# Gated mix of a 2D spectral filter and a Mish MLP: W read once and copied on chip, loads on three queues, half of w1 ahead of later x, larger butterflies, new cost numbers in its build-time planner

## Chip, cores and metric

The kernel runs on one core of a Trainium2 chip. The metric is device microseconds of one execution, as the median of several runs. The profile's span is 1.7 us shorter than the time of the same run (164.8 against 166.51 us before). Runs of this one-core program are called fast or slow by their time against the fastest of the same kernel; each run also lists the mean granted TensorE clock.

## Reference

Input x is 2048 x 512 in bf16. The output is `g * a + (1 - g) * b`:

```python
g = sigmoid((x * gate_w).sum(-1, keepdims=True))
a = irfft2(rfft2(x) * (w_r + 1j * w_i))            # W is 2048 x 257, real and imaginary
b = mish(x @ w1 + b1) @ w2                         # w1 512 x 1792, w2 1792 x 512
# reference() takes B_x too, but calls the MLP with A_x
```

## The kernel before

All transforms are matmuls. x is transposed on TensorE (`tr`), butterflies (sums and differences of halves of a tile) on VectorE or GpSimd feed the row transform (`a1`, with matrix FD), the first column stage (`s1`, with FT) follows, and its result goes through DRAM scratch `scr1` (four writes `r1w`, four reads `r1r`) to be regrouped. Then comes the second stage `s2`, the product with W on VectorE, and the way back (SM, GT and GD are the matrices of these stages). A DMA is issued by an engine into its own queue: `sp` is SyncE, `act` ScalarE, `pool` GpSimd. The MLP is `mm1` (56 groups of four 512-column matmuls, the activation function Mish on ScalarE after each) and `mm2`.

Nothing is ordered at run time. Each step is a task; a small planner in the kernel simulates the engines at build time with cost numbers and a priority per task, and writes one fixed instruction list per engine. Each engine works through its list in order. If the planner believes that W arrives early, it places W's first use early, and TensorE then stands still there.

```python
free = {e: 0.0 for e in ENGS}                       # in schedule(): when each engine is free
...
def dma(name, dst, src, nbytes, ..., queue="sp", bw=DMA_BW):       # DMA_BW = 390e3 bytes/us
    t = G.add(name, [(queue, 0.1, lambda e: e.dma_start(dst, src))], ...)   # an issue costs 0.1 us
    t.xfer = nbytes / bw                            # all transfers one after the other
...
# W into Wa/Wb [128, 32, 257]: both halves of the partitions hold the same values
def wload(nm, dst, src_t, o, cos, wdep):
    for co in (cos,):
        base = 64 * co
        ...  # p: 32 rows of 16448 B; r, n, s: rows of 514 B in reversed order
for t in range(NT):
    ...
    if t % 4 == 3:
        t_r1w.append(dma(f"r1w{t // 4}", scr1_w[...], A1s[...], ...))
        wload(*((("wr", Wa, ...), ("wi", Wb, ...))[t // 8]), (t // 4) % 2, list(t_r1w[-1].deps))
...
G.add("tab", ..., reads=WA + WB + ["SM"], ...)      # first TensorE use of W
G.add("z", ..., reads=IN2 + ["SM"], ...)            # needs all four scr1 reads
G.add(f"s2_{gp}", ..., reads=[("In2", gp // 4), "SM"], ...)   # needs one of them
G.add(f"hs_{c}_{ft}", ..., reads=[sl, "b1f", "gth"], ...)     # Mish only after the gate
```

## Time and profile before

| | before |
|---|---|
| timed, first three runs | 168.49 us (167.88 to 169.06) |
| profiled span | 164.8 us |
| TensorE busy | 137.2 us |
| longest TensorE wait | 13.89 us |
| DMA bytes | 22.78 MB |

From the page of the profile, the busy tenths of TensorE, the granted TensorE clock in tenths and the DMA engines' share, each in 40 slices of 4.12 us:

```profile
PE   1397998693002999999999999999999999999991
PEclk9999999999655699999999999999999999999999
DMA  4798999999999993030303891100101000011011
```

TensorE has a hole in slices 10 to 13 and is full afterwards, so I read the kernel's end as TensorE's remaining work plus whatever idle time came before. The clock falls inside the hole and comes back only with the work after it. DMA is busy from about 6 to 60 us.

The timeline of TensorE (start in us, duration, engine, line, operation and tiles, count, and in brackets the idle time before and what ended it). L785 is mm1, L687 the first use of W, L733 the first use of scr1:

```profile
30.70 7.94 PE L785 MATMUL ps<-xT,w_sb 128*128 128x512 bf16 x36 [1.39 <-ACT hsb L793]
52.54 0.22 PE L687 MATMUL ps<-Wa,SM 128*128 128x32 bf16 x1 [13.89 <-DMA Wb<-in_A_w_i_dram]
...
53.21 0.39 PE L733 MATMUL ps<-R,SM 128*128 128x256 bf16 x1 [0.19 <-DMA R<-scr]
```

36 matmuls are 9 mm1 groups; 4 more stood earlier. So 13 groups were done ahead of W's first use, and 43 of the 56 were still to come while TensorE waited. W came at 52.5 us, the first scr1 read at 53.2: both arrive together, so with this order, taking away only one of the two waits should gain next to nothing.

The same trace, SyncE's DMA issues from 28 us (the duration is the time the issue took):

```profile
28.23 0.47 SPq L480 DMA_DIRECT2D scr<-R  x1
28.74 6.41 SPq L480 DMA_DIRECT2D Wb<-in_A_w_i_dram  x4
...
36.18 0.36 SPq L480 DMA_DIRECT2D scr<-R  x1
36.59 7.71 SPq L480 DMA_DIRECT2D Wb<-in_A_w_i_dram  x4
45.83 1.81 SPq L480 DMA_DIRECT2D R<-scr  x4
```

The last scr1 write was issued at 36.18 us although its data was ready at 30.2: four Wb loads were before it in the list. The table of stretches (start:end, length, busy time and count of each engine, clock, DMA share, GB/s):

```profile
42.00:48.00 6.00, 0.00 (x0) 0.00 (x0) 0.00 (x0) 0.00 (x0) 0.00 (x0) 0.53 1.09 272
48.00:54.00 6.00, 1.08 (x10) 0.85 (x12) 0.38 (x2) 0.00 (x0) 0.00 (x0) 0.50 1.13 256
54.00:60.00 6.00, 5.97 (x27) 2.71 (x27) 4.23 (x14) 2.55 (x4) 0.00 (x0) 0.83 1.06 371
```

No engine computes from 42 to 48 us.

### The profile page before, as it was taken

What the parts mean: (1) busy time and instruction counts of PE and PEld (TensorE: products, weight loads), DVE (VectorE), ACT (ScalarE), POOL (GpSimd) and SP (SyncE); (2) the same over time, 40 slices, a digit from 0 to 9 for tenths busy, and PEclk for the clock granted to TensorE, in tenths of its full rate; (3) what the DMA queues carried; (4) which work ended last, traced back from release to release, by engine and by line L of the source; (5) the groups of instructions that cost most, each with busy time, mean ns of one, the idle gap of its engine ahead of it and who ended that gap; (6) DMA issues with size and microseconds to landing.
All of it is one profiled execution on the core that took longest, in us unless ns stands there. A gap on an engine that the chain in (4) does not pass through costs nothing.

```text
span 164.8 us, 2256 instructions
## 1 busy us (share of the span) xinstructions
PE 137.2 (83%) x835; PEld 72.3 (44%) x850; DVE 74.5 (45%) x172; ACT 76.4 (46%) x126; POOL 9.3 (6%) x16
## 2 busy tenths in 40 slices
PE   1397998693002999999999999999999999999991
PEld 0265667241001444444444475544566444444440
DVE  0288796300000869599630079207888500311311
ACT  3259876984000277865232768622359774000000
POOL 1082063000000000000000000000000000000000
PEclk9999999999655699999999999999999999999999
DMA  4798999999999993030303891100101000011011
GB/s 144 282 374 336 248 157 342 153 280 139 344 135 282 385 354 118 38 127 0 127 0 142 242 258 64 64 4 0 64 0 66 4 0 0 0 64 64 4 64 64
DMA packets 19615, 22.78 MB, mean 138 GB/s; under 512 B 916, under 2 KB 16404, under 8 KB 19476
## 3 DMA queue, kind: packets, MB, share of 16 engines
q1 hardware_dynamic: 19604, 22.63, 49.8%
q8 instruction: 7, 0.11, 0.3%
q14 instruction: 4, 0.03, 0.1%
HBM read 16.34 MB, written 6.29 MB: 137 GB/s over the span
## 4 chain that ended last, share of the span: by engine, by line
PE 76%; DMA 13%; ACT 4%; POOL 2%; issue 1%; SPq 1%; DVE 0%; POOLq 0%
PE ps L803 29%; PE ps L785 28%; DMA scr<-R 6%; DMA R<-scr 4%; PE ps L851 4%; DMA R<-in_A_x_dram 3%; PE ps L832 2%; PE ps L759 2%; PE ps L760 2%; PE ps L735 2%; PE ps L582 2%; ACT R L505 2%; POOL PX L602 1%; PE ps L659 1%; PE ps L637 1%
## 5 line engine op out<-in xcount | busy, mean ns | idle before, releaser
L785 PE MATMUL ps<-xT,w_sb 128*128 128x512 bf16 x220 | 53.5, 382 | 1.7 <-ACT hsb L793 1.4
L793 ACT ACTIVATE hsb<-ps,b1f 128x512 bf16<-128x512 f32 x56 | 37.9, 688 | 30.5 <-PE ps L785 30.1
L803 PE MATMUL ps<-w_sb,hsb 128*128 128x512 bf16 x218 | 49.7, 379 | 0.3
L803 PEld LDWEIGHTS ps<-w_sb,hsb 128*128 128x128 bf16 x224 | 21.8, 98 | 25.5
L785 PEld LDWEIGHTS ps<-xT,w_sb 128*128 128x128 bf16 x224 | 21.5, 99 | 24.1 <-ACT hsb L793 1.7
L505 ACT ACTIVATE R<-ps 128x512 bf16<-128x512 f32 (+1 forms) x29 | 16.8, 594 | 7.7 <-PE ps L760 5.0
L882 DVE SCALAR_TENSOR_TENSOR R<-ps,omg,R 128x512 bf16<-128x512 f32 x8 | 6.0, 751 | 26.0 <-PE ps L803 26.0
L504 DVE CAST R<-ps 128x512 bf16<-128x512 f32 (+1 forms) x19 | 12.8, 689 | 9.1 <-PE ps L760 6.2
L746 DVE TENSOR_TENSOR PX<-ps,Wa 128x256 bf16<-128x256 f32 x32 | 12.0, 416 | 0.6 <-PE ps L734 0.6
L582 PE MATMUL ps<-ident,R 128*128 128x128 bf16 x64 | 6.7, 264 | 6.6 <-DMA R<-in_A_x_dram 6.5
L746 DVE TENSOR_TENSOR PX<-ps,Wb 128x256 bf16<-128x256 f32 x32 | 12.0, 417 | 0.1
L687 PE MATMUL ps<-Wa,SM 128*128 128x32 bf16 x1 | 0.2, 217 | 13.9 <-DMA Wb<-in_A_w_i_dram 13.9
L813 ACT ACTIVATE R<-ps,omg 128x512 bf16<-128x512 f32 x8 | 5.5, 687 | 12.1 <-PE ps L803 12.1
L694 DVE COPY tz<-ps 128x64 f32<-128x64 f32 x1 | 0.2, 225 | 22.8 <-PE ps L690 22.8
L591 ACT ACTIVATE xT<-ps 128x512 bf16<-128x512 bf16 x12 | 6.6, 601 | 6.3 <-PE ps L582 6.2
L839 DVE CAST TT<-ps 128x512 bf16<-128x512 f32 x5 | 3.4, 690 | 12.9 <-PE ps L832 12.9
L851 PE MATMUL ps<-GD,TT 128*128 128x256 bf16 x64 | 9.1, 273 | 0.0
L859 DVE SCALAR_TENSOR_TENSOR PX<-ps,gcol,R 128x512 f32<-128x512 f32 x8 | 6.0, 744 | 6.8 <-ACT R L813 6.1
L582 PEld LDWEIGHTS ps<-ident,R 128*128 128x128 bf16 x64 | 5.1, 119 | 8.0 <-DMA R<-in_A_x_dram 7.0
L874 DVE SCALAR_TENSOR_TENSOR R<-ps,gcol,PX 128x256 bf16<-128x256 f32 x16 | 7.7, 482 | 1.2 <-ACT PX L865 0.8
L875 DVE SCALAR_TENSOR_TENSOR R<-ps,ngcol,PX 128x256 bf16<-128x256 f32 x16 | 7.6, 476 | 0.0
L851 PEld LDWEIGHTS ps<-GD,TT 128*128 128x128 bf16 x64 | 5.9, 98 | 3.6 <-ACT TT L842 1.3
(88 smaller groups left out, 105.9 us busy)
## 6 DMA issues: line engine op xcount, KB each, us to landing
scr<-R SPq DMA_DIRECT2D x8, 512.0 KB, 3.1
R<-scr SPq DMA_DIRECT2D x8, 512.0 KB, 7.4
w_sb<-in_B_w_dram SPq DMA_DIRECT2D x4, 896.0 KB, 11.8
out_dram<-R SPq DMA_DIRECT2D x8, 256.0 KB, 2.0
R<-in_A_x_dram SPq DMA_DIRECT2D x3, 512.0 KB, 6.5
Wa<-in_A_w_r_dram SPq DMA_DIRECT2D x2, 514.0 KB, 9.5
Wb<-in_A_w_i_dram SPq DMA_DIRECT2D x2, 514.0 KB, 11.2
SM<-c_sm SPq DMA_DIRECT2D x1, 640.0 KB, 8.8
```

Of the source, the lines that this page charges most:

```text
L504: G.add(name, [("dve", dve_dur(n), lambda e: e.tensor_copy(out=outf(), in_=inf())), ("act", act_dur(n), lambda e: e.activation(outf(), inf ...
L505: ("act", act_dur(n), lambda e: e.activation(outf(), inf(), AF.Copy))],
L582: ins = e.transpose(psb[:, bk(sl), 128 * dt_:128 * (dt_ + 1)], x_sb[:, t, 128 * dt_:128 * (dt_ + 1)], ident[:, :])
L591: return e.activation(xT[:, :, t, :], psb[:, bk(sl), 0:512].rearrange("p (a b) -> p a b", a=4), AF.Copy)
L746: ins = e.tensor_tensor(out=po, in0=px, in1=pw, op=ALU.mult)
L785: ins = e.matmul(ps[:, bk(sl), :], w1_sb[:, dt_, 128 * ft:128 * (ft + 1)], xT[:, dt_, 4 * c:4 * c + 4, :], start=(dt_ == 0), stop=(dt_ == 3))
L793: return e.activation(hsb[:, hb, ft, :], ps[:, bk(sl), :], AF.Mish, bias=b1f[:, ft:ft + 1])
L803: ins = e.matmul(ps[:, bk(sl), :], hsb[:, hb, ft, 128 * tl:128 * (tl + 1)], w2_sb[:, ft, :], start=(ft == 0), stop=(ft == NFT - 1))
L851: ins = e.matmul(ps[:, bk(sy), 256 * hh:256 * (hh + 1)], TT[:, st.i, i, :], GD[:, i, :], start=(i % 2 == 0), stop=(i % 2 == 1))
L859: return e.scalar_tensor_tensor(out=o, in0=ps[:, bk(sy), 0:256].unsqueeze(1).to_broadcast([128, 2, 256]), scalar=gcol[:, t:t + 1], in1=ya[ ...
L874: e.scalar_tensor_tensor(out=ya[:, t, 0:256], in0=ps[:, bk(sy), 256:512], scalar=gcol[:, t:t + 1], in1=tE[:, se.i, 0:256], op0=ALU.mult, o ...
L875: return e.scalar_tensor_tensor(out=ya[:, t, 256:512], in0=ps[:, bk(sy), 256:512], scalar=ngcol[:, t:t + 1], in1=hi, op0=ALU.mult, op1=ALU ...
```

## The change

The intent: read W from HBM once (2.1 instead of 4.2 MB) into partitions 0 to 63 and copy it to 64 to 127 on chip; put W, the stage matrices SM, w2, GD and GT on the GpSimd queue, so that scr1's writes don't stand behind them; split the first loads over SyncE and ScalarE; load half of w1 ahead of x's later tiles so that mm1 can start; make most butterflies over four tiles instead of two. The planner's cost numbers change too.

```diff
+BGRP = {1: (0, 2), 3: (2, 2), 7: (4, 4), 11: (8, 4), 15: (12, 4)}
-        free = {e: 0.0 for e in ENGS}
+        free = {e: 0.8 for e in ENGS}
-            t = G.add(name, [(queue, 0.1, lambda e: e.dma_start(dst, src))], ...
+            t = G.add(name, [(queue, {"sp": 0.46, "act": 0.46, "pool": 1.0}[queue], lambda e: ...)], ...
+        ld_x(0, 1)
+        dma("ld_fd", ..., queue="act")
+        ld_x(1, 4)
+        dma("ld_ft0", ..., queue="act")
+        ld_w1(0)
...  (b1, gate_w on "act"; then x 4 to 8, FT, x 8 to 16 on SyncE)
+        t_w1 = ld_w1(1)
+        def wload(nm, dst, src_t, o):       # partitions 0 to 63 only, deps=[t_w1], queue="pool"
...  (the rows of 514 B are planned with bw=130e3)
+        dma("ld_sm", ..., deps=[t_w1], queue="pool")    # likewise w2 and GD; GT after the last s1
+        for o, W in (("Wa", Wa), ("Wb", Wb)):
+            for h in range(2):
+                js = slice(16 * h, 16 * h + 16)
+                G.add(f"cp{o}{h}", [("dve", dve_dur(4112, 4), ... e.tensor_copy(out=W[64:128, js, :], in_=W[0:64, js, :])),
+                                    ("act", act_dur(4112), ...)], ...)
-            if t % 2 == 1:                  # butterflies over two tiles
+            if t in BGRP:
-                wload(*(...)[t // 8]), (t // 4) % 2, list(t_r1w[-1].deps))
```

More of the change, by code (lines that the diff above doesn't have):

```diff
@@ L17 @@
 NEARLY = 8
+BGRP = {1: (0, 2), 3: (2, 2), 7: (4, 4), 11: (8, 4), 15: (12, 4)}
+BIDX = {t: i for i, t in enumerate(BGRP)}
 KOFF = (0, 2, 1, 3)
@@ L387, in schedule @@
         return order
-PR = dict(ld=100.0, tr=97.0, a1=98.0, s1=99.0, mid=96.0, fin=94.0, mm1=80.0, act=90.0, mm2=70.0, out=95.0, gate=96.5)
+PR = dict(ld=100.0, tr=97.0, a1=98.0, s1=99.0, mid=96.0, fin=94.0, mm1=80.0, act=90.0, mm2=70.0, out=95.0, gate=96.5, cp=95.5)
 def _build(nc, A_x, A_w_r, A_w_i, B_w1, B_b1, B_w2, gate_w, out):
@@ L479, in dma @@
         def dma(name, dst, src, nbytes, reads=(), writes=(), deps=(), is_out=False, prio=None, queue="sp", bw=DMA_BW):
-            t = G.add(name, [(queue, 0.1, lambda e: e.dma_start(dst, src))], reads=reads, writes=writes,
-                      deps=deps, prio=PR["ld"] if prio is None else prio)
+            t = G.add(name, [(queue, {"sp": 0.46, "act": 0.46, "pool": 1.0}[queue], lambda e: e.dma_start(dst, src))],
+                      reads=reads, writes=writes, deps=deps, prio=PR["ld"] if prio is None else prio)
             t.xfer = nbytes / bw
@@ L515, in _build @@
         t_x = []
-        groups = [(0, 1), (1, 4), (4, 8), (8, 12), (12, 16)]
-        for gi, (a, b) in enumerate(groups):
-            t_x.append(dma(f"ld_x{gi}", x_sb[:, a:b, :], xv[:, a:b, :], 128 * 1024 * (b - a),
-                           writes=[("x", i) for i in range(a, b)]))
-            if gi == 0:
-                dma("ld_fd", FD[:], d_c["FD"][:], 128 * 1536, writes=["FD"])
-            if gi == 1:
-                dma("ld_ft0", FT[:, 0:4, :], d_c["FT"][:, 0:4, :], 128 * 1024, writes=[("FT", 0)])
-            if gi == 2:
-                dma("ld_ft1", FT[:, 4:16, :], d_c["FT"][:, 4:16, :], 128 * 3072, writes=[("FT", 1), ("FT", 2), ("FT", 3)])
-                dma("ld_b1", bgraw[0:14, :], B_b1.rearrange("(ft p) -> ft p", p=128), 3584, writes=["braw"])
-                dma("ld_gw", bgraw[14:18, :], gate_w.rearrange("(dt p) -> dt p", p=128), 1024, writes=["gwraw"])
@@ L528, in _build, with ld_x, ld_w1 @@
-        for h in range(2):
-            dma(f"ld_w1_{h}", w1_sb[:, :, 896 * h:896 * (h + 1)], w1v[:, :, 896 * h:896 * (h + 1)],
-                128 * 4 * 1792, writes=[("w1", h)])
+        def ld_x(a, b, queue="sp"):
+            t_x.append(dma(f"ld_x{a}", x_sb[:, a:b, :], xv[:, a:b, :], 128 * 1024 * (b - a), writes=[("x", i) for i in range(a, b)], queue=queue))
+        def ld_w1(h):
+            return dma(f"ld_w1_{h}", w1_sb[:, :, 896 * h:896 * (h + 1)], w1v[:, :, 896 * h:896 * (h + 1)], 128 * 4 * 1792, writes=[("w1", h)])
@@ new lines, in _build @@
+        ld_x(0, 1)
+        dma("ld_fd", FD[:], d_c["FD"][:], 128 * 1536, writes=["FD"], queue="act")
+        ld_x(1, 4)
+        dma("ld_ft0", FT[:, 0:4, :], d_c["FT"][:, 0:4, :], 128 * 1024, writes=[("FT", 0)], queue="act")
+        ld_w1(0)
+        dma("ld_b1", bgraw[0:14, :], B_b1.rearrange("(ft p) -> ft p", p=128), 3584, writes=["braw"], queue="act")
+        dma("ld_gw", bgraw[14:18, :], gate_w.rearrange("(dt p) -> dt p", p=128), 1024, writes=["gwraw"], queue="act")
+        ld_x(4, 8)
@@ new lines, in _build, with back @@
+        dma("ld_ft1", FT[:, 4:16, :], d_c["FT"][:, 4:16, :], 128 * 3072, writes=[("FT", 1), ("FT", 2), ("FT", 3)])
+        ld_x(8, 12)
+        ld_x(12, 16)
+        t_w1 = ld_w1(1)
+        def wload(nm, dst, src_t, o):
+            v = src_t.rearrange("(g h e2 j) k -> g h e2 j k", g=16, h=2, e2=2)
+            dma(f"ld_{nm}p", dst[0:32, :, :].rearrange("p j k -> p (j k)"), v[:, 0, :, :, :].rearrange("g e2 j k -> g e2 (j k)"),
+                32 * 16448, writes=[(o, 0)], deps=[t_w1], queue="pool")
+            nb = dst[32:64, :, :]
+            row = nb.ap[0][0]
+            def back(part, j, npart, nj, pstep):
+                return bass.AP(nb.tensor, nb.offset + part * row + j * 257, [[pstep * row, npart], [-257, nj], [1, 257]])
+            n1 = bass.AP(src_t.tensor, src_t.offset + 65 * 257, [[128 * 257, 16], [257, 32], [1, 257]])
+            dma(f"ld_{nm}r", back(0, 31, 16, 32, 2), n1, 16 * 32 * 514, writes=[(o, 1)], deps=[t_w1], queue="pool", bw=130e3)
+            n0 = bass.AP(src_t.tensor, src_t.offset + 97 * 257, [[128 * 257, 16], [257, 31], [1, 257]])
+            dma(f"ld_{nm}n", back(1, 31, 16, 31, 2), n0, 16 * 31 * 514, writes=[(o, 2)], deps=[t_w1], queue="pool", bw=130e3)
+            s64 = bass.AP(src_t.tensor, src_t.offset + 64 * 257, [[128 * 257, 16], [1, 257]])
+            dma(f"ld_{nm}s", nb[1:32:2, 0, :], s64, 16 * 514, writes=[(o, 3)], deps=[t_w1], queue="pool", bw=130e3)
@@ new lines, in _build @@
+        wload("wr", Wa, A_w_r, "Wa")
+        wload("wi", Wb, A_w_i, "Wb")
+        dma("ld_sm", SM[:], d_c["SM"][:], 128 * 2 * 128 * len(MATS), writes=["SM"], deps=[t_w1], queue="pool")
+        for h in range(2):
+            dma(f"ld_w2_{h}", w2_sb[:, 7 * h:7 * (h + 1), :], w2v[:, 7 * h:7 * (h + 1), :], 128 * 7 * 1024,
+                writes=[("w2", h)], deps=[t_w1], queue="pool")
+        dma("ld_gd", GD[:], d_c["GD"][:], 128 * 2048, writes=["GD"], deps=[t_w1], queue="pool")
+        for o, W in (("Wa", Wa), ("Wb", Wb)):
+            for h in range(2):
+                js = slice(16 * h, 16 * h + 16)
+                G.add(f"cp{o}{h}", [("dve", dve_dur(4112, 4), lambda e, W=W, js=js: e.tensor_copy(out=W[64:128, js, :], in_=W[0:64, js, :])),
+                                    ("act", act_dur(4112), lambda e, W=W, js=js: e.activation(W[64:128, js, :], W[0:64, js, :], AF.Copy))],
+                      reads=[(o, i) for i in range(4)], writes=[(o, 4, h)], prio=PR["cp"])
@@ L533, in _build @@
+        WA = [("Wa", i) for i in range(4)] + [("Wa", 4, h) for h in range(2)]
+        WB = [("Wb", i) for i in range(4)] + [("Wb", 4, h) for h in range(2)]
         sl = fslot()
@@ L546, in _build @@
         wl = []
-        def wload(nm, dst, src_t, o, cos, wdep):
-            for co in (cos,):
-                base = 64 * co
-                v = src_t.rearrange("(g h e2 j) k -> g h e2 j k", g=16, h=2, e2=2)
-                wl.append(dma(f"ld_{nm}p{co}", dst[base:base + 32, :, :].rearrange("p j k -> p (j k)"),
-                              v[:, 0, :, :, :].rearrange("g e2 j k -> g e2 (j k)"), 32 * 16448,
-                              writes=[(o, co, 0)], deps=wdep))
-                nb = dst[base + 32:base + 64, :, :]
-                row = nb.ap[0][0]
-                def back(part, j, npart, nj, pstep):
-                    return bass.AP(nb.tensor, nb.offset + part * row + j * 257, [[pstep * row, npart], [-257, nj], [1, 257]])
-                n1 = bass.AP(src_t.tensor, src_t.offset + 65 * 257, [[128 * 257, 16], [257, 32], [1, 257]])
-                wl.append(dma(f"ld_{nm}r{co}", back(0, 31, 16, 32, 2), n1, 16 * 32 * 514,
-                              writes=[(o, co, 1)], deps=wdep))
-                n0 = bass.AP(src_t.tensor, src_t.offset + 97 * 257, [[128 * 257, 16], [257, 31], [1, 257]])
-                wl.append(dma(f"ld_{nm}n{co}", back(1, 31, 16, 31, 2), n0, 16 * 31 * 514,
-                              writes=[(o, co, 2)], deps=wdep))
-                s64 = bass.AP(src_t.tensor, src_t.offset + 64 * 257, [[128 * 257, 16], [1, 257]])
-                wl.append(dma(f"ld_{nm}s{co}", nb[1:32:2, 0, :], s64, 16 * 514,
-                              writes=[(o, co, 3)], deps=wdep))
-        WA = [("Wa", c, i) for c in range(2) for i in range(4)]
-        WB = [("Wb", c, i) for c in range(2) for i in range(4)]
         t_tr, t_a1, t_s1, t_r1w, t_s1e = [], [], [], [], []
@@ L593, in _build @@
             G.add(f"evx{t}", [("dve", 0.43, f_evx), ("act", 0.6, f_evx_a)], reads=[sl], writes=[("xT", t)], prio=PR["tr"] + 0.2)
-            if t % 2 == 1:
-                t0 = t - 1
-                hv = (t // 2) % 2
-                xss = xs[:, hv, :, :].rearrange("p j (t s) -> p j t s", t=4)[:, :, 0:2, :]
-                def mk(fname, o, a, b, op):
-                    def f(e):
-                        return e.tensor_tensor(out=o, in0=a, in1=b, op=op)
-                    return f
-                tr_ = slice(t0, t0 + 2)
-                ff = mk("d", XB[:, 2:4, tr_, :], xT[:, 0:2, tr_, :], xT[:, 2:4, tr_, :], ALU.subtract)
-                G.add(f"bd{t}", [("dve", dve_dur(512, 2), ff), ("pool", pool_dur(512), ff)],
-                      reads=[("xT", t0), ("xT", t)], writes=[("XB", 1, t)], prio=PR["a1"])
-                ff = mk("s", xss, xT[:, 0:2, tr_, :], xT[:, 2:4, tr_, :], ALU.add)
-                G.add(f"bs{t}", [("dve", dve_dur(512, 2), ff), ("pool", pool_dur(512), ff)],
-                      reads=[("xT", t0), ("xT", t)], writes=[("xs", hv)], prio=PR["a1"])
-                ff = mk("r0", XB[:, 0, tr_, :], xss[:, 0], xss[:, 1], ALU.add)
-                G.add(f"br0{t}", [("dve", dve_dur(256, 2), ff), ("pool", pool_dur(256), ff)],
-                      reads=[("xs", hv)], writes=[("XB", 0, t)], prio=PR["a1"])
-                ff = mk("r2", XB[:, 1, tr_, :], xss[:, 0], xss[:, 1], ALU.subtract)
-                G.add(f"br2{t}", [("dve", dve_dur(256, 2), ff), ("pool", pool_dur(256), ff)],
-                      reads=[("xs", hv)], writes=[("XB", 2, t)], prio=PR["a1"])
@@ new lines, in _build, with bfly @@
+            if t in BGRP:
+                t0, n = BGRP[t]
+                hv = BIDX[t] % 2
+                xss = xs[:, hv, :, 0:128 * n].rearrange("p j (t s) -> p j t s", t=n)
+                tr_ = slice(t0, t0 + n)
+                def bfly(nm, o, a, b, op, cols, reads, writes):
+                    ff = lambda e: e.tensor_tensor(out=o, in0=a, in1=b, op=op)
+                    G.add(f"{nm}{t}", [("dve", dve_dur(cols, 2), ff), ("pool", pool_dur(cols), ff)], reads=reads, writes=writes, prio=PR["a1"])
+                xr = [("xT", i) for i in range(t0, t0 + n)]
+                bfly("bd", XB[:, 2:4, tr_, :], xT[:, 0:2, tr_, :], xT[:, 2:4, tr_, :], ALU.subtract, 256 * n, xr, [("XB", 1, t)])
+                bfly("bs", xss, xT[:, 0:2, tr_, :], xT[:, 2:4, tr_, :], ALU.add, 256 * n, xr, [("xs", hv)])
+                bfly("br0", XB[:, 0, tr_, :], xss[:, 0], xss[:, 1], ALU.add, 128 * n, [("xs", hv)], [("XB", 0, t)])
+                bfly("br2", XB[:, 1, tr_, :], xss[:, 0], xss[:, 1], ALU.subtract, 128 * n, [("xs", hv)], [("XB", 2, t)])
@@ L628, in f_a1 @@
                 return e.matmul(o[:, :, 1, :], XB[:, 1, t, :], f2(128), start=True, stop=True)
-            to = t | 1
+            to = min(i for i in BGRP if i >= t)
             t_a1.append(G.add(f"a1_{t}", [("pe", pe_dur(256, 2) + pe_dur(128, 2), f_a1)],
@@ L645, in _build @@
                                  reads=[("A1s", i) for i in range(a, a + 4)], writes=[("scr1", t // 4)], prio=PR["ld"] + 1))
-                wload(*((("wr", Wa, A_w_r, "Wa"), ("wi", Wb, A_w_i, "Wb"))[t // 8]), (t // 4) % 2, list(t_r1w[-1].deps))
-                if t == 3:
-                    dma("ld_sm", SM[:], d_c["SM"][:], 128 * 2 * 128 * len(MATS), writes=["SM"], deps=t_r1w[-1].deps)
-        dma("ld_gt", GT[:], d_c["GT"][:], 128 * 4096, writes=["GT"], deps=t_s1)
+        dma("ld_gt", GT[:], d_c["GT"][:], 128 * 4096, writes=["GT"], deps=t_s1, queue="pool")
         sl_g = fslot()
@@ L673, in _build @@
                 reads=[("scr1", i) for i in range(4)], writes=[("In2", h)], deps=t_tr, prio=PR["ld"] + 1)
-        for h in range(2):
-            dma(f"ld_w2_{h}", w2_sb[:, 7 * h:7 * (h + 1), :], w2v[:, 7 * h:7 * (h + 1), :], 128 * 7 * 1024,
-                writes=[("w2", h)], deps=t_r1w)
-        dma("ld_gd", GD[:], d_c["GD"][:], 128 * 2048, writes=["GD"], deps=t_r1w)
         sl_t = fslot()
```

## The prediction

> **What bounds the kernel now.** The profiled span is 164.8 us (timed median 168.49, about 3.7 more). From 54 us on TensorE is full (table of stretches: 5.97 of 6, 5.95 of 6, then 99%). The chain of waits ends on mm2 (29%) and mm1 (28%); after 137 us only mm2 is left, so the spectral branch is done long before the end. The end time is TensorE's work plus its idle time before 54 us. Of that, 13.89 us is one wait (timeline: 38.64 to 52.54, ended by the last Wb load). Work resumes at half clock (0.50 granted in 48 to 54 us, 0.83 in 54 to 60), an estimated 1.5 us lost. Some 8.7 us more is scattered over the first 30 us, 5.4 of it before 6 us, waiting for x.
>
> Why W is late: DMA is busy without a break from 6 to 60 us, all loads on one queue. The last scr1 write's data is ready at 30.2 us, but its issue stands behind Wb loads until 36.18 and it lands 9.57 us later; the reads back are issued at 45.83 and land at 53.2.
>
> **What the change does.** It removes half of the W traffic, 2.1 of 4.2 MB. From 16.5 to 53.6 us the DMAs moved about 8.6 MB at 231 GB/s, against 357 in the load phase; charging other bytes at 357 leaves about 190 GB/s for W, so about 11 us of DMA time goes. It adds four copies of 64 x 4112 elements, estimated from the bf16 DVE copy (512 in 0.42 us) at 1.5 to 3.5 us each, on a DVE idle from 30 to 53 us: off the path. W, SM, w2, GD and GT leave SyncE, so scr1 writes issue when ready. The Trainium skill ("DMA: Bandwidth & Descriptors", "Issuing engines are not separate DMA queues") says that all queues run on the same 16 engines and interleave: I count no extra bandwidth, only no queueing behind W. w2 and GD now compete with the scr1 reads (up to 5 us given back).
>
> Estimated: w1 landed at 17, W at 32 to 34, SM 34 to 36; last scr1 write issued 30 to 32, landed 35; reads landed 42 to 46. From 31 us TensorE can fill with mm1: two chunks hold over 20 us of it. The order on each engine is fixed at build time; with issue costs now near the measured 0.43 us I expect more mm1 ahead of the spectral work. The 13.9 us gap shrinks to 0 to 6, most likely 3, and the half clock, which the trace shows only after that gap, mostly goes.
>
> Head: x1 to x3 land about 0.4 us earlier. Half of w1 (0.9 MB, 2.5 us at 357 GB/s) delays x4 and later, but four mm1 groups fill that wait. GpSimd loses butterflies to DVE; fewer, larger ones repay it. Net -1 to +1 us.
>
> **Sum.** 168.5 - 10.5 (gap) - 1.0 (clock) + 0 (head) = 157.0 us; range 152 to 163. Faster by over 2%: 0.91; within: 0.06; slower: 0.03.
>
> **What would show it.** Right: no TensorE wait over 6 us after 30 us; last scr1 write issued within 1 us of its data; reads landed by 46; DMA bytes 20.6 to 20.8 MB; TensorE busy 135 to 137 us. Wrong: a longer wait for W, SM or the copies, or low clock after 30 us.
>
> **What would make it wrong.** GpSimd's many 514 B rows go out slowly, or start late behind all of w1, and the fixed order uses W too early: the gap stays, 163 or more. GpSimd blocked on that wait holds butterflies. Scr1 reads share engines with w2 and land near 50. On the other side, no gap and a better filled head give 152.

## The result

The changed kernel took 153.37 us (153.04 to 154.86, 4 runs) against 168.66 (4 runs of before). The ratio of fast runs is 0.9116, 95% interval 0.9047 to 0.9184. All ratios here are the mean time of one kernel's fast runs over that of the other's of the same rounds, so not quite the ratio of the medians quoted. The profiled span is 151.8 us: 13.0 less (the times differ by 15.3, because before's profiled run, 166.51 us, was 2 us faster than its median). DMA bytes are 20.68 MB.

The page of the kernel after, the same three lines (slices of 3.8 us):

```profile
PE   0479998979999999999999999999999999999990
PEclk9999998799999999999999999999999999999999
DMA  4999399999993920303030399013010000101011
```

The hole is gone, not smaller. The timeline of TensorE (L785 mm1, L687 W's first use, L733 scr1's first use):

```profile
32.25 1.04 PE L785 MATMUL ps<-xT,w_sb 128*128 128x512 bf16 x4 [0.96 <-ACT hsb L793]
...
33.80 6.54 PE L785 MATMUL ps<-xT,w_sb 128*128 128x512 bf16 x28
40.17 0.22 PE L687 MATMUL ps<-Wa,SM 128*128 128x32 bf16 x1
...
40.51 10.52 PE L785 MATMUL ps<-xT,w_sb 128*128 128x512 bf16 x48
51.01 0.28 PE L733 MATMUL ps<-R,SM 128*128 128x256 bf16 x1
```

With the 4 groups done earlier this is 12 mm1 groups ahead of W's first use and 24 ahead of scr1's first use, where before had 13 ahead of both. And scr1's first use starts at 51.0 us against 53.2: the spectral data arrive hardly earlier. SyncE's issues from 34 us say so too:

```profile
34.91 5.79 SPq L484 DMA_DIRECT2D scr<-R  x1
46.97 1.75 SPq L484 DMA_DIRECT2D R<-scr  x4
```

The last scr1 write starts when its data is ready (the last cast ends at 34.83 us), but its issue takes 5.79 us and it lands 12.0 us after the start of its issue; the reads are issued at 46.97, later than before's 45.83.

The DMA view of 34 to 40 us shows why. It lists packets, MB and share of the 16 DMA engines for each queue; software_dynamic is here GpSimd's queue (W, SM, w2, GD, GT), hardware_dynamic SyncE's (scr1):

```profile
q0 software_dynamic: 549, 2.07, 87.1%
q1 hardware_dynamic: 549, 0.28, 15.6%
```

Both queues sent the same number of packets, but SyncE's held 512 bytes and GpSimd's 3.8 KB on average, so the scr1 writes got 0.28 of 2.35 MB, an eighth. The rerun shows the same (551 against 550 packets), and so does e5 below (806 against 806 from 36 to 50 us). From 24 to 30 us, with the second scr1 write already issued, it was even less, 24 packets against 233; why is open. The second and third writes, issued at 23.83 and 30.28 us, took 20.2 and 15.1 us to land, where the last three took 8.5 to 9.6 us in before, in one queue with W. These two and the last write all landed only after GpSimd's last load (GT, issued at 34.52, landed 9.3 us later). No run changed the queue or the packet size alone, so this is read from traces and not tried.

So a kernel that finishes 13 us sooner by the profile has its critical data 2.2 us sooner. What changed is what TensorE did meanwhile. The table of stretches:

```profile
24.00:30.00 6.00, 5.89 (x89) 4.43 (x90) 4.94 (x10) 2.63 (x8) 0.46 (x1) 0.72 1.03 170
...
42.00:48.00 6.00, 6.00 (x29) 2.74 (x28) 0.00 (x0) 4.77 (x8) 0.00 (x0) 1.00 0.60 178
48.00:54.00 6.00, 6.00 (x32) 2.81 (x30) 2.56 (x8) 3.93 (x7) 0.00 (x0) 1.00 0.93 340
```

TensorE is full at full clock in the stretches that were empty. One new thing: the clock column shows 0.72 for 24 to 30 us, where TensorE was busy 5.89 of 6 us.

### The profile page after: what moved, and what is told of

It reads as the page before. It is cut to its first block, busy times and chain, and to the rows that moved or that the text cites. A ratio compares the mean times of both kernels' runs of the same rounds, so it can differ in the third digit from the quotient of the medians.

```text
span 151.8 us, 2262 instructions
## 1 busy us (share of the span) xinstructions
PE 139.3 (92%) x850; PEld 73.0 (48%) x850; DVE 79.6 (52%) x173; ACT 75.5 (50%) x125; POOL 11.1 (7%) x21
## 2 busy tenths in 40 slices
DMA packets 14207, 20.68 MB, mean 136 GB/s; under 512 B 788, under 2 KB 10420, under 8 KB 14132
## 4 chain that ended last, share of the span: by engine, by line
PE 86%; ACT 6%; DMA 4%; DVE 2%; issue 0%; SPq 0%; DVEq 0%
PE ps L803 32%; PE ps L785 31%; PE ps L851 5%; DMA R<-in_A_x_dram 4%; ACT R L509 3%; PE ps L832 2%; PE ps L598 2%; PE ps L759 2%; PE ps L735 2%; PE ps L760 2%; PE ps L633 2%; PE ps L634 1%; ACT hsb L793 1%; PE ps L664 1%; PE ps L645 1%; ACT L793 1%
## 5 line engine op out<-in xcount | busy, mean ns | idle before, releaser
L785 PE MATMUL ps<-xT,w_sb 128*128 128x512 bf16 x224 | 52.8, 383 | 1.1 <-ACT hsb L793 1.0
L803 PE MATMUL ps<-w_sb,hsb 128*128 128x512 bf16 x224 | 51.0, 379 | 0.0
L793 ACT ACTIVATE hsb<-ps,b1f 128x512 bf16<-128x512 f32 x56 | 37.9, 689 | 11.5 <-PE ps L785 11.1
L785 PEld LDWEIGHTS ps<-xT,w_sb 128*128 128x128 bf16 x224 | 21.3, 99 | 25.4 <-ACT hsb L793 2.3
L509 ACT ACTIVATE R<-ps 128x512 bf16<-128x512 f32 (+1 forms) x27 | 15.6, 595 | 13.6 <-PE ps L760 7.1
L508 DVE CAST R<-ps 128x512 bf16<-128x512 f32 (+1 forms) x21 | 14.0, 689 | 11.6 <-PE ps L760 6.4
L746 DVE TENSOR_TENSOR PX<-ps,Wa 128x256 bf16<-128x256 f32 x32 | 11.9, 414 | 10.8 <-PE ps L734 10.5
L598 PE MATMUL ps<-ident,R 128*128 128x128 bf16 x64 | 5.8, 247 | 6.1 <-DMA R<-in_A_x_dram 6.0
L842 ACT ACTIVATE TT<-ps 128x512 bf16<-128x512 f32 x13 | 7.5, 593 | 4.9 <-PE ps L832 3.2
L607 ACT ACTIVATE xT<-ps 128x512 bf16<-128x512 bf16 x11 | 5.8, 612 | 4.2 <-PE ps L598 4.1
L839 DVE CAST TT<-ps 128x512 bf16<-128x512 f32 x3 | 2.0, 685 | 9.5 <-PE ps L832 9.5
L633 PE MATMUL ps<-FD,R 128*128 128x256 bf16 x16 | 5.4, 341 | 1.1 <-DVE R L618 1.1
```

Source lines behind the costliest of these rows:

```text
L508: G.add(name, [("dve", dve_dur(n), lambda e: e.tensor_copy(out=outf(), in_=inf())), ("act", act_dur(n), lambda e: e.activation(outf(), inf ...
L509: ("act", act_dur(n), lambda e: e.activation(outf(), inf(), AF.Copy))],
L598: ins = e.transpose(psb[:, bk(sl), 128 * dt_:128 * (dt_ + 1)], x_sb[:, t, 128 * dt_:128 * (dt_ + 1)], ident[:, :])
L633: e.matmul(o[:, :, 2:4, :], XB[:, 2, t, :], f4(256), start=True, stop=False)
L746: ins = e.tensor_tensor(out=po, in0=px, in1=pw, op=ALU.mult)
L785: ins = e.matmul(ps[:, bk(sl), :], w1_sb[:, dt_, 128 * ft:128 * (ft + 1)], xT[:, dt_, 4 * c:4 * c + 4, :], start=(dt_ == 0), stop=(dt_ == 3))
```

## Experiments

Theory A: the gain is TensorE's order. The new planner numbers put more mm1 ahead of the spectral work, and it fills the wait. Theory B: the gain is the transfers, W halved and moved to another queue. Twelve runs were made, eleven new kernels and after once more; all were correct. The first four shared one chip and three rounds, in which before ran unsteadily (165.77 to 201.07, five of seven runs slow), so their intervals are wide and their verdict by rule is "unclear", although all four intervals lie below 0.984. Their yardstick is before's two fast runs, 165.77 and 167.78 us; in the other groups before's median was 167.91 to 169.08. So these four ratios are, if anything, too high beside the others. The others had five rounds.

| run | W read | planned order | mm1 groups ahead of W / of scr1 | median us | ratio to before (95%) |
|---|---|---|---|---|---|
| before | twice | old | 13 / 13 | 168.66 | 1 |
| e1 | twice | new numbers | 25 / 26 | 155.8 | 0.9325 (0.9168 to 0.9481) |
| e3 | twice | mm1 forced first, `z` in front | 28 / 28 | 161.14 | 0.9622 (0.9405 to 0.9838) |
| e3b | twice | mm1 forced first | 28 / 28 | 159.37 | 0.9408 (0.9358 to 0.9459) |
| e4 | once | old numbers | 8 / 12 | 159.63 | 0.9563 (0.9403 to 0.9723) |
| e9 | once | mm1 forced first | 28 / 28 | 153.78 | 0.8992 (0.8941 to 0.9042) |
| after (run again) | once | new numbers | 12 / 24 | 153.16 | 0.9130 (0.9091 to 0.9170) |
| e2 | once (as after) | old numbers | 7 / 16 | 160.46 | 0.9635 (0.9486 to 0.9784) |
| e5 | twice (rest as after) | new numbers | 25 / 28 | 158.79 | 0.9385 (0.9344 to 0.9426) |
| e10 | once (as after) | pushed further | 12 / 28 | 151.51 | 0.8998 (0.8972 to 0.9024) |
| e6 | once (as after), old first loads | new numbers | 9 / 21 | 155.49 | 0.9271 (0.9231 to 0.9312) |
| e7 | once (as after), two-tile butterflies | new numbers | 8 / 22 | 156.65 | 0.9327 (0.9280 to 0.9374) |
| e8 | once (as after), warm-up matmuls | new numbers | 12 / 24 | 154.73 | 0.9152 (0.9105 to 0.9198) |

### e1_numbers: only the planner's numbers, on the kernel before

```diff
-        free = {e: 0.0 for e in ENGS}
+        free = {e: 0.8 for e in ENGS}
-            t = G.add(name, [(queue, 0.1, ...
+            t = G.add(name, [(queue, 0.46, ...
-  ... writes=[(o, co, 1)], deps=wdep))
+  ... writes=[(o, co, 1)], deps=wdep, bw=130e3))      # rows of 514 B; likewise n and s
```

> The kernel before with all its transfers unchanged (W still read twice, all on one queue); only the cost numbers of its build-time planner are those of the change, so that 26 mm1 groups instead of 13 stand ahead of the first spectral matmul. Theory A (the gain is the order of TensorE's instructions): the 13.9 us wait shrinks to about 3 us, time 155 to 159. Theory B (the gain is the W traffic and the queues): 166 to 169.

Measured: 155.8 us (154.13 to 156.34), in theory A's range. The trace of this run, TensorE:

```profile
30.88 18.30 PE L785 MATMUL ps<-xT,w_sb 128*128 128x512 bf16 x83 [1.39 <-ACT hsb L793]
52.58 0.22 PE L687 MATMUL ps<-Wa,SM 128*128 128x32 bf16 x1 [3.39 <-DMA Wb<-in_A_w_i_dram]
```

W arrives at 52.58 us, within 0.04 us of before. No byte was saved and the wait fell from 13.89 to 3.39 us. SyncE's list of transfers is the same as in before. Order alone, with every transfer as before, gives most of the gain. Which of the three changed numbers does it was not run; building the kernel before with one at a time puts 13 / 13 groups ahead with `free`, 13 / 14 with the issue cost and 25 / 26 with `bw=130e3`, so here it is the rate of the 514-byte rows.

### e2_old_numbers: the kernel after, with the old planner numbers

```diff
-        free = {e: 0.8 for e in ENGS}
+        free = {e: 0.0 for e in ENGS}
-  {"sp": 0.46, "act": 0.46, "pool": 1.0}[queue]
+  0.1
-  ..., bw=130e3)
+  ...)
```

> The kernel after with all its transfers; only the planner's numbers are those of before, so that 7 mm1 groups stand ahead of W's first use and 16 ahead of the first scr1 use. Theory A: TensorE waits about 6 us for the W copies near 34 to 40 us and 3 to 4 us for the reads near 51, time 160 to 164. Theory B: 152 to 156, as after.

Measured: 160.46 us. The time falls in theory A's range, but not for the reason expected. GpSimd's timeline of this run:

```profile
15.94 2.51 POOL L484 DMA_DIRECT2D Wa<-in_A_w_r_dram  x4 [6.08 <-DMA w_sb<-in_B_w_dram]
...
23.30 0.59 POOL L484 DMA_DIRECT2D GD<-c_gd  x1
23.90 2.27 POOL L618 TENSOR_TENSOR R<-PX 128x512 bf16<-128x512 bf16 x2
```

and TensorE's:

```profile
26.27 0.27 PE L633 MATMUL ps<-FD,R 128*128 128x256 bf16 x1 [4.38 <-POOL R L618]
```

The planner thought that a GpSimd DMA issue costs 0.1 us, so it left butterflies on GpSimd behind all twelve of them, which held the engine from 15.94 to 23.89 us; TensorE waited 4.38 us for a butterfly. The expected wait at W did not appear, because everything before it came later; the wait at scr1 was 1.10 us.

### e3_mm1_first and e3b_mm1_first: the kernel before, mm1 forced ahead by dependences

```diff
+        last = mm1 group 28
+        for n in ["tab", "z"] + [f"s2_{g}" for g in range(16)]:
+            by[n].deps.append(last)
+        # mm2 of the first chunk behind s2i_0
+        by["z"].deps.append(by["s2i_3"])        # e3b only
```

> The kernel before, transfers and planner numbers untouched; only extra dependences at build time put 28 mm1 groups ahead of the spectral matmuls. Theory A: no wait over 3 us near 52 us, perhaps 2 to 3 us for w2 near 58; time 154 to 158. Theory B: 166 to 169.

> The kernel of the third run with one dependence more: the two small matmuls that need all four scr1 reads stand behind the fourth spectral group instead of in front, which cost 5.4 us there. W twice, one queue, old numbers. If the order alone explains the gain: no TensorE wait over 2 us between 31 and 60 us, full clock, 153 to 156. If the traffic is needed too: 157 or more.

Measured: 161.14 and 159.37 us. e3 lies between the ranges of the two theories; e3b misses the range for order alone and lies in the one for "the traffic is needed too". Both traces show a wait that the edit created. In e3, `z`, which needs all four scr1 reads, now stood first:

```profile
58.17 0.22 PE L701 MATMUL ps<-R,SM 128*128 128x32 bf16 x1 [5.41 <-DMA R<-scr]
```

In e3b the wait for W is 0.27 us, as wanted, but mm1 was used up and mm2 came before w2, whose load stands behind W and scr1 in the one queue:

```profile
61.77 2.32 PE L803 MATMUL ps<-w_sb,hsb 128*128 128x512 bf16 x7 [3.23 <-DMA w_sb<-in_B_w_dram]
```

So theory A in its pure form falls: filling by mm1 ends, and what has to be there by then (W, all reads, w2) is a matter of transfers.

### e4_w_once: the kernel before, W read once and copied, old queue and old numbers

```diff
-                wload(*(...)[t // 8]), (t // 4) % 2, list(t_r1w[-1].deps))
+                if t % 8 == 3:
+                    wload(nm, W, src, o, 0, list(t_r1w[-1].deps))
+                    for h in range(2):
+                        G.add(f"cp{o}{h}", ...)      # the copies of the change
```

> The kernel before with W read once and copied on chip, still on the one queue and with the old planner numbers (8 mm1 groups ahead of W's first use, 12 ahead of scr1's). Theory B: the scr1 reads land about 10 us earlier than in before (near 43 us) and most of the gain comes, 154 to 158. Theory A: arrival does count where the order is too early, but the wait stays near 5 to 8 us, 158 to 163.

Measured: 159.63 us. The scr1 reads were issued at 42.03 us instead of 45.83 and first used at 46.28 instead of 53.21. SyncE's issues:

```profile
33.20 0.36 SPq L480 DMA_DIRECT2D scr<-R  x1
42.03 1.76 SPq L480 DMA_DIRECT2D R<-scr  x4
```

So with half of W and everything in one queue, the scr1 reads are issued 4.9 us earlier than in after with its GpSimd queue (46.97). In time, e2, which has after's queues and head and the old numbers too, is no faster than e4 (159.91 to 161.93 against 159.02 to 160.15, same chip and rounds), though e2 also carries its 4.38 us wait.

Theory B's range is missed by 1.6 us. Theory A's holds in time, but not its wait of 5 to 8 us; TensorE's longest waits after the head were shorter (total, times, longest):

```profile
PE ps L792 <- ACT hsb L800: 2.4, 1, 2.4
PE ps L637 <- DVE R L504: 2.2, 1, 2.2
PE ps L694 <- DVE Wb L651: 1.6, 1, 1.6
```

The 2.2 us come from the copies themselves: the planner put the Wa copy (2.36 us for both halves) ahead of a cast that TensorE needed, and VectorE had to wait for Wa at 28.2 us. Off the critical path is a property of the order too. Still, with the old numbers, halving W gave 4.4%, although the planner then put fewer mm1 groups ahead (8 / 12 instead of 13 / 13).

### e9_once_mm1_first: e4 with the order of e3b

```diff
+        # e3b's dependences, and
+        for n in ("cpWa0", "cpWa1", "cpWb0", "cpWb1"):
+            by[n].deps.append(by["e2_15"])      # copies behind the last cast
```

> The same TensorE order as in the run beside it, but W read once and copied on chip, still on the one queue; the copies stand behind the last cast. If traffic buys nothing once the order is right: within 1 us of that run, 153 to 156, although the scr1 reads are issued near 42 instead of 46 us. If it does buy something: 2 us or more below that run.

Measured: median 153.78 us, in two groups: 151.78, 151.92 and 152.38 at a mean clock of 0.998 to 1.0, and 155.18 to 155.74 at 0.978. The profile fell in the second group and is not used for times; it has no TensorE wait over 0.5 us from 34 to 60 us, and the reads were issued at 43.27 us. Against e3b (0.9408) the ratio is 0.8992: transfers do buy something once the order is right. e3b had no run at clock 1.0, so part of that difference may be clock; but e9's three runs at 0.978, too, lie below every run of e3b (157.58 to 160.91). The w2 wait that e9 doesn't have was 3.23 us. e9 also moved the copies, so its list is not e3b's in every place. Its ratio all but equals that of e10 (0.8998), the best kernel with three queues.

### e5_w_twice: the kernel after, W read twice

```diff
-        def wload(nm, dst, src_t, o):
+        def wload(nm, dst, src_t, o):
+          for co in range(2):                  # both halves from HBM, still the GpSimd queue
-        for o, W in (("Wa", Wa), ("Wb", Wb)): ...   # copies
```

> The kernel after with W read twice from HBM on the GpSimd queue and no copies; the planner sees it and puts 25 mm1 groups ahead of W's first use, 28 ahead of the first scr1 use. Order theory: TensorE stays full, W lands near 45, the reads near 58, waits of 0 to 4 us, 153 to 157. Traffic theory: the 11 us of DMA time come back, 161 or more.

Measured: 158.79 us, 2 us outside the order theory's range and 2 us short of the traffic theory's. The planner saw the longer loads, and TensorE did not wait for W at all. It did wait for scr1, whose reads were issued at 58.37 us:

```profile
62.41 0.28 PE L729 MATMUL ps<-R,SM 128*128 128x256 bf16 x1 [3.50 <-DMA R<-scr]
```

Inside the kernel after, reading W once instead of twice is worth about 2.8% (0.9385 against 0.9116 and 0.9130), the change of order that the planner makes with it (12 / 24 against 25 / 28) included.

### e6_old_loads and e7_twos: the head of the change, undone in two parts

```diff
# e6: all first loads on SyncE, x ahead of w1, as before
# e7:
-BGRP = {1: (0, 2), 3: (2, 2), 7: (4, 4), 11: (8, 4), 15: (12, 4)}
+BGRP = {t: (t - 1, 2) for t in range(1, 16, 2)}
```

> The kernel after, unchanged, as the yardstick for the two runs beside it: 152.5 to 155.

> The kernel after with its first loads as in before: all on the SyncE queue, all of x ahead of w1. If the new load order is worth something: 1.5 us or more slower than after. The forecast gave the head -1 to +1 us. The trace of after showed x landing later (first transposes at 4.64 us against 3.07, the last cast before the scr1 write at 34.8 against 30.2), so I expect the same or up to 2 us faster: 151.5 to 154.

> The kernel after with the butterflies in groups of two tiles as in before. Four-tile groups save about 0.07 us per instruction pair on DVE (0.69 us for 1024 columns against twice 0.42) but make TensorE wait for four tiles. I expect the same within 1 us: 152.5 to 154.5.

The 0.07 us in the third text is per two-tile instruction (0.42 us against half of 0.69). Measured in the same rounds: after 153.16, e6 155.49 (ratio to before 0.9271), e7 156.65 (0.9327). Both expectations missed (after's own held): both parts are worth something, 1.5% and 2.2% of after. For e6 the trace shows where. x does come earlier (first transposes at 2.99 us against 4.20 in the profile of after beside it), but the planner then put the gate behind the last column stage, and ScalarE's Mish, which needs the gate, started with TensorE empty:

```profile
33.38 6.87 PE L784 MATMUL ps<-xT,w_sb 128*128 128x512 bf16 x19 [3.03 <-ACT hsb L792]
```

In after the same wait is 0.96 to 0.99 us. That this is an effect of order and not of the loads was not isolated by a run. For e7 the only profile is of a slow run (161.77 us), so its cause stays open.

### e8_warm: matmuls ahead of the first transpose

```diff
+            for _ in range(32):
+                ins = e.matmul(ps[:, bk(sl_w), 0:128], ident[:, :], ident[:, :], start=True, stop=True)
```

> The kernel after with 32 matmuls of 128 columns on the identity tile ahead of the first transpose, into a bank that is overwritten later; they end before x lands. In after, TensorE ran at half rate until 14.5 us (a 256-column matmul took 0.42 us against 0.27). If that half rate costs: the first FD matmuls take 0.27 us, 150 to 152.5. If loads and casts set the pace there: 153 to 154.

Measured: 154.73 us (153.93 to 155.69): no gain, and 0.7 us above the second range, so neither expectation held in time. TensorE in this run:

```profile
1.44 3.59 PE L524 MATMUL ps<-ident 128*128 128x128 bf16 x32 [1.44 <-POOL ident L514]
...
7.06 0.84 PE L608 MATMUL ps<-ident,R 128*128 128x128 bf16 x12 [1.75 <-DMA R<-in_A_x_dram]
10.37 0.37 PE L643 MATMUL ps<-FD,R 128*128 128x256 bf16 x1 [2.47 <-DVE R L628]
10.54 0.42 PE L644 MATMUL ps<-FD,R 128*128 128x256 bf16 x1
```

The 12 transposes ran in 0.84 us instead of 1.46, so the clock was up at 7 us. They only waited longer afterwards (2.47 us for the butterfly), and at 10.5 us the 256-column matmul took 0.42 us again. Warming up before a stretch that data arrival paces gained nothing here.

### e10_more_mm1: the order pushed further in the kernel after

The second profile of after (the rerun) has a wait that the first had not:

```profile
50.69 0.28 PE L733 MATMUL ps<-R,SM 128*128 128x256 bf16 x1 [2.37 <-DMA R<-scr]
```

Its clock stayed at 1.00 from 24 to 30 us, so TensorE got to the scr1 matmuls sooner and waited there. Both runs took the same time (153.50 and 153.11 us).

```diff
+        by["z"].deps.append(by["s2i_2"])
+        for n in [f"s2_{g}" for g in range(16)]:
+            by[n].deps.append(mm1 group 28)
+        # mm2 of the first chunk behind s2i_0
```

> The kernel after with the order pushed further: 28 instead of 24 mm1 groups ahead of the first scr1 use, the two small matmuls behind the third spectral group, mm2 of the first chunk behind the first spectral group. In the second profile of after TensorE waited 2.37 us for the scr1 reads at 50.7 us, in the first not at all (it had lost as much to the low clock before). If order is what is left there: no wait near 50 us, 151 to 153, best times below 152.5. If work moved in front only makes a gap later (mm1 of the second chunk is then used up): 153 to 155.

Measured: 151.51 us; the fast runs are 150.79 to 151.81, ratio to before 0.8998 (0.8972 to 0.9024), below after's 0.9130 with intervals that don't touch. Its profile (of a slow run, 153.6 us) shows no wait near 50 us. All six fast runs beat every run of after. This version beats both kernels.

## Why the prediction was right or wrong

The time was right: 153.37 us inside 152 to 163, faster as forecast; the change was 15.3 us where 11.5 was forecast. Point by point:

- **"The end time is TensorE's work plus its idle time before 54 us."** Right in the main: e1 took away 10.5 us of that wait and its span fell by 10.4. But in e3, e3b and e5 the wait came later, at 58 to 62 us, and e7's time is not explained by any trace of a fast run.
- **"The 13.9 us gap shrinks to 0 to 6, most likely 3."** Right, at the good end: no wait for W or scr1 in one profile of after (the longest wait after 30 us, 0.96 us, is for the Mish), 2.37 us in the other. This term of the sum (10.5) was under-sized by 1 to 3 us.
- **"The half clock ... mostly goes."** Right after 30 us (1.00 in every stretch). That it comes only after such a gap was wrong: one profile of after has 0.72 in 24 to 30 us without a gap.
- **"Last scr1 write issued 30 to 32, landed 35; reads landed 42 to 46."** Wrong, and it is the step that failed. It was issued at 34.9 us, 0.08 us after its data as the check demanded, but landed at 46.9; the reads were issued at 46.97 and first used at 51.0. I took SyncE's list for the cause of the lateness. The step was "only no queueing behind W". In after that list is free and the write still needs 12 us, while w2, GD and GT go out on the other queue. The Trainium skill ("DMA: Bandwidth & Descriptors", "Issuing engines are not separate DMA queues") says that transfers from all queues run on the same 16 engines and interleave. The trace agrees: 549 packets of each queue from 34 to 40 us. I used this for the bandwidth but not for the write's own delay. From 34 to about 45 us the engines were busy almost without a break at 361 to 395 GB/s (table of stretches), about 4 MB, and three scr1 writes, 1.5 MB in 512-byte packets, were waiting: by the equal counts they took turns with the loads they had been freed from, packet by packet, and came out last. e4, with the same bytes of W in one queue, had its reads issued at 42.03. Which of those loads costs how much was not tried.
- **The sum, for all that.** Data 5 to 9 us later than forecast hardly hurt, because the filling with mm1, which the prediction named but did not size, reached to 51 us, and because the head gained where nothing was forecast. That the total fell in the range is in part luck.
- **"From 31 us TensorE can fill with mm1."** Right, and it carried the result; it was given a sentence where the W traffic was given a paragraph. The prediction put the new order down to issue costs alone; building after without the row rate puts 12 / 20 groups ahead, without the issue costs 7 / 22, so both count there. e1 shows it: W at 52.58 us as before, the wait 3.39 instead of 13.89 us.
- **"About 11 us of DMA time goes."** Not tested as a size; what it is worth was tested. Inside after it is worth 2.8% (e5), with the old numbers 4.4% (e4), and with mm1 forced first it is the difference between 0.9408 and 0.8992. Neither theory is the whole: order alone 6.8%, traffic with the old numbers 4.4%, and the whole change 8.8%, less than the sum, which fits that both take away the same wait.
- **"Head: net -1 to +1 us."** Mis-sized. x1 to x3 came 0.4 us later, not earlier (their transposes start at 6.66 us against 6.24; those of the first tile at 4.64 against 3.07), yet undoing the load order costs 1.5% and undoing the four-tile butterflies 2.2%. The term should have been a gain of 2.3 and 3.5 us, each taken together with the order that follows from it; that the two add was not tried.
- **Copies "off the path".** Right in after, and over-sized (2.37 and 2.35 us for two each, so 1.2 us for one, against 1.5 to 3.5). e4 shows that it need not be.
- **GpSimd blocked on DMA issues "holds butterflies".** It did not happen in after; it did in e2, 4.38 us, with a planner that did not know the cost.
- **What would show it.** DMA bytes (20.68 MB), the longest wait after 30 us and the write's issue held. Reads landed by 46 did not (first used at 51.0), nor did TensorE busy of 135 to 137 us: it was 139.3. Before's 137.2, on which that range seems to rest, lacks 15 matmul records (835 against after's 850).

## What to carry to other kernels

When an engine with a fixed instruction list waits for data, ask first what other work could stand in front of the wait: moving 12 mm1 groups (e1, 154.13 to 156.34 us) was worth more here than halving the transfer (e4, 159.02 to 160.15, same rounds). A build-time planner with wrong costs is a performance bug: measure a DMA issue and a row-wise load in the trace and give it those numbers. Filling has an end, so the data must come within the filler; after that, traffic counts again. A second queue does not put a transfer in front: here two queues sent packets in equal numbers, so the one with 512-byte packets lost. Before moving a transfer, compare its packet size with that of what will run beside it.

## What the Trainium skill lacked or had wrong

- "TensorE: Matmul & The Clock Gate" ("Why this matters for your kernels" and "HAM oscillation") gives avoiding idle gaps over about 3 us as the rule for keeping full clock. Here the clock fell without one. In the first profile of after the longest TensorE idle time from 10 to 26 us was 0.71 us, just ahead of the gate's 64 one-column matmuls; then 256-column matmuls took 0.42 us:

```profile
24.10 1.80 PE L664 MATMUL ps<-gw_sb,xT 128*128 128x1 bf16 x64 [0.71 <-ACT xT L607]
...
25.92 0.42 PE L634 MATMUL ps<-FD,R 128*128 128x256 bf16 x1
```

  In the rerun of the same kernel they took 0.27 us after the same gate:

```profile
22.67 1.75 PE L664 MATMUL ps<-gw_sb,xT 128*128 128x1 bf16 x64 [0.70 <-ACT xT L607]
...
24.39 0.27 PE L634 MATMUL ps<-FD,R 128*128 128x256 bf16 x1
```

  The page's "second HAM failure mode" speaks of frequent micro-idles between groups of matmuls; a run of very short matmuls as a cause is not on it, and is only suspected here, since no run took the gate away.
- The same page's advice to warm up (for measuring) says nothing of the case here: e8 warmed TensorE up ahead of a stretch that waits 1.75 and 2.47 us for data, and it was at half rate again at 10.5 us, with no gain in time.
- "DMA: Bandwidth & Descriptors" ("SWDGE vs HWDGE vs iDMA") says that descriptors for GpSimd's queue are made by software on GpSimd. The trace fits, and adds the price, which no page gives for such a list: twelve issues held GpSimd for 7.9 us (16.53 to 24.45 us in after; about 0.6 us each for W, 1.0 for a half of w2). They stand in one list with its own compute: in e2 a butterfly started only after the last of them, and TensorE waited 4.38 us for it.
- "DMA: Bandwidth & Descriptors" says that an engine takes turns between queues packet by packet, but has no figure for how a transfer then fares when another queue is full. Here 549 packets (as the trace counts them) of 512 B went out beside 549 of 3.8 KB, an eighth of the bytes; a 512 KB write took 5.79 us to issue and 12.0 us to land, an earlier one 20.2 us; and the first x tile took 3.8 us (3.3 in the rerun) instead of 2.2 with FD on a second queue beside it and x1 to x3 and w1 right behind.
